# Pairs 4 and 5 in the form of the later pairs, in a kernel of chunked attention and a gated feed-forward layer

## The chip, the cores and the metric

One core of one Trainium2 chip. The metric is the device time in microseconds, the median of several executions. The engines are named as in the profile: PE multiplies matrices, PEld loads its weights, DVE, ACT and POOL work on vectors, and SP here only issues DMA transfers.

## The reference

The first part is a recurrence over a sequence (4 batches, 8 heads, 768 steps, head size 32, state size 16). The second part is a feed-forward layer on its output (256 in, 1536 inside, 256 out, 3072 tokens).

```python
for c in range(nc):                                   # chunks of the sequence
    cum = np.cumsum(la, axis=-1)                      # la = log(a) of the chunk
    L = np.exp(cum[..., :, None] - cum[..., None, :]) * causal
    M = np.einsum('bhin,bhjn->bhij', Cc, Bc) * L
    y_intra = np.einsum('bhij,bhjd->bhid', M, xc)
    y_inter = np.einsum('bhin,bhnd->bhid', Cc, state) * np.exp(cum)[..., None]
    y[:, :, sl] = y_intra + y_inter
    Bx = np.einsum('bhjn,bhjd->bhjnd', Bc, xc) * decay_from_j[..., None, None]
    state = decay_full[..., None, None] * state + np.sum(Bx, axis=2)
...
gate = np.maximum(x @ w_gate, 0.0)                    # x: y as (3072, 256)
return (gate * (x @ w_val)) @ w_out
```

## The kernel before

**Tiles.** The kernel cuts the sequence into chunks of 128 steps, six in a batch, and takes two chunks as a pair: 12 pairs of 256 tokens, three in a batch. A batch boundary lies ahead of pairs 3, 6 and 9. Two pairs are one block of 512 tokens for the feed-forward part, so there are six blocks. The decay of `a` is not put into the matrix: B is divided and C multiplied by the running product of `a` since the batch's middle (`fac`, and `wfac` for the first four pairs). What is carried over that point is multiplied by `over`.

**One pair.** B and C are loaded (`bcr`), x is loaded (`xr`) and cast (`xb`, `to_x`). Then come these steps:

- G: C times B for each head, into four PSUM banks; `gevac` masks it and writes it to SBUF (`gs`). For this B and C must lie with the state on the partitions, that is, turned.
- the states: B times x, summed over the chunks (`A_ps`, the PSUM bank with the tag `Aps`).
- `inter`: the carried term, C times the state, into y.
- `Dm`: `gs` times x, added into the same y. `yevac` writes y to `yT`, the input of the feed-forward part.

**Three forms.** Pairs 0 to 3 are wide (`NWIDE`): a load takes two neighbouring steps at once, B and C are scaled into `bs` (`scale_bc`), PE turns them (`turn`), ACT and DVE copy the result (`tevac`), and B is turned back (`back`). Pairs 4 and 5 are scaled into `bs` too and turned by PE, in the plain order of steps. Their states come from `states`, which adds up in PSUM, and `spread_one` on DVE multiplies out each chunk's carried term. Pairs 6 to 11 take a third form (`NDMA = 6`): POOL scales B and C into one of three zero-padded buffers (`scale_padded`: one product, two copies), and a DMA transpose that SP issues turns them into `TT`. `G_rows` and `inter_rows` read `TT` in strips of 32 rows. `states_two` makes the states of two pairs. `sums_two` adds them up chunk by chunk: a sum on DVE (`run`, L708 or L710), then a product on POOL (`Sn`, L717). At the fourth chunk of a batch (`c % NC == NC - 3`) POOL first multiplies the sum by `over` (L713), and the next sum on DVE adds that result:

```python
if c % NC == NC - 3:
    past = att.tile([128, 64], FP32, tag="run", name="run", bufs=4)
    nc.gpsimd.tensor_scalar_mul(past, total, over2[:, c // NC:c // NC + 1])
    total = past
running[:] = [total]
```

**Order.** Each engine, and SP's and POOL's DMA queues too, takes its instructions in the order in which the program writes them (`in_order`). The loop over blocks (L963) writes that order by hand. In block `b`, `P = 2b + 2` and `Q = 2b + 3` are the pairs of the next block, whose attention is worked on while block `b`'s feed-forward part runs. `gv` makes one of 12 slices of gate and value for 512 tokens (L738); ACT applies relu (L741) and DVE multiplies (L742). `gvh` does the same for 256 tokens (L753, L760, L763), so that a block can start while its second pair is not done: blocks 0, 1 and 2 do their first 4, 6 and 8 slices in halves. `fout` makes the output of 128 tokens from the 12 slices (L783), and `foevac` copies and stores it. With `apart` set, `fout` puts its first bank where `A_ps` lies (tag `Aps`, one buffer). From block 2 on the tail is the third form: `fout` 9 slices, `G_rows(P)`, `inter_rows`, and so on, down to `Dm_two` and `states_two` of the next two pairs. Blocks 0 and 1 have tails of their own.

**Loads.** SP issues nearly all of them, in program order: C, B and x of a pair by `load`. `held` and the memsets on `bcr` or `xr` make a load wait until DVE comes to them. `bcr` and `xr` have four buffers each, `TT` four, `xb` six.

Of the kernel before, what the change touches and what calls it, by code (L numbers as in the profile page):

```python
# [29 lines left out]
def kernel(  # L30
# [84 lines left out]
    even = const.tile([128, 24], FP32)  # L115
    even_att = att.tile([128, 32], FP32, bufs=1)
# [136 lines left out]
    over2 = const.tile([128, NB], FP32)  # L253
# [6 lines left out]
    def over_sum(de):  # L260
        own = smask.rearrange("p t (q d) -> p (t q) d", q=4)[:, :, 0]
        prod = const.tile([128, NB, 8], FP32)
        nc.vector.tensor_tensor(
            out=prod, in0=de.rearrange("p (b h) -> p b h", b=NB),
            in1=own.rearrange("p (o h) -> p o h", o=1).to_broadcast([128, NB, 8]),
            op=ALU.mult)
        nc.vector.tensor_reduce(out=over, in_=prod, op=ALU.add, axis=mybir.AxisListType.X)

    def over_sum2(de):
        own = smask.rearrange("p t (q d) -> p q t d", q=4)[:, :, :, 0]  # L270
        prod = const.tile([128, 2, 8], FP32)
        for n in range(2):
            nc.vector.tensor_tensor(
                out=prod[:, n].rearrange("p (q t) -> p q t", t=2),
                in0=de[:, (2 + n) * 8:(3 + n) * 8].rearrange("p (q t) -> p q t", t=2),
                in1=own, op=ALU.mult)
        nc.vector.tensor_reduce(out=over2[:, 2:4], in_=prod, op=ALU.add,
                                axis=mybir.AxisListType.X)
# [4 lines left out]
    NDMA = 6  # L283
# [24 lines left out]
    def new_bs(p):  # L308
        st[p]["bs"] = att.tile([128, 4, 128], BF16, tag="bs", name="bs", bufs=6)
        bs = st[p]["bs"]  # L310
        if p < NWIDE:
            st[p]["tin"] = [[bs[:, 2 * j + r] for r in range(2)] for j in range(2)]
        else:
            st[p]["tin"] = [[bs[:, 2 * i + j] for i in range(2)] for j in range(2)]
            st[p]["B"] = st[p]["tin"][0]
# [4 lines left out]
    def views(p, js):  # L320
        s = st[p]
        dst = s["bs"].rearrange("s k (q t n) -> s k t q n", q=4, t=2)
        if p < NWIDE:
            ks = slice(2 * js.start, 2 * js.stop)
            src = s["bcr"].rearrange("s (t q) j r n -> s (j r) t q n", t=2)
            return src[:, ks], dst[:, ks]
        return s["bcr"].rearrange("s i j (t q) n -> s (i j) t q n", t=2), dst

    def cast_bc(p, eng, js):
        src, dst = views(p, js)  # L330
        for t in range(2):
            copy(eng, dst[:, :, t], src[:, :, t])

    def scale_bc(p, eng, js=slice(0, 2), f=None, ts=(0, 1)):
        b, c0, _ = place(p)
        src, dst = views(p, js)
        if f is None:
            if p < NWIDE:
                f = wfac[:, p, js].rearrange("s j r h -> s (j r) h")
            else:  # L340
                f = fac[:, b, c0:c0 + 2].rearrange("s c j h -> s (c j) h")
        n = f.shape[1]
        for t in ts:
            eng.tensor_tensor(  # L344
                out=dst[:, :, t], in0=src[:, :, t],
                in1=f[:, :, 4 * t:4 * t + 4].to_broadcast([128, n, 4, N]), op=ALU.mult)

    def scale_one(p, eng, j):

        b, c0, _ = place(p)  # L350
        for i in range(2):
            f = fac[:, b, c0 + i, j].rearrange("s (t q) -> s t q", t=2)
            eng.tensor_tensor(
                out=st[p]["bs"][:, 2 * i + j].rearrange("s (q t n) -> s t q n", q=4, t=2),
                in0=st[p]["bcr"][:, i, j].rearrange("s (t q) n -> s t q n", t=2),
                in1=f.to_broadcast([128, 2, 4, N]), op=ALU.mult)

    def to_x(p, eng, f=None):
        xb = att.tile([128, 2 * NH * D], BF16, tag="xb", name="xb", bufs=6)
        xr = st[p]["xr"].rearrange("s i h d -> s (i h) d")  # L360
        out = xb.rearrange("s (k d) -> s k d", d=D)
        if f is None:
            copy(eng, out, xr)
        else:
            eng.tensor_tensor(out=out, in0=xr, in1=f.to_broadcast([128, 2 * NH, D]),
                              op=ALU.mult)
        st[p]["x"] = [xb[:, i * NH * D:(i + 1) * NH * D] for i in range(2)]

    def scale(p, eng):
        if p >= NDMA:  # L370
            scale_padded(p, eng)
        else:
            new_bs(p)
            scale_bc(p, eng)
        to_x(p, eng)
# [15 lines left out]
    def bevac(p, eng):  # L391
# [3 lines left out]
        if p < NWIDE:  # L395
            src = src.rearrange("s r m -> s m r")
            dst = dst.rearrange("s (m r) -> s m r", r=2)
        else:
            src = src.rearrange("s i m -> s (i m)")
        copy(eng, dst, src)  # L400
# [16 lines left out]
    def ct(p, i, rows=slice(0, 128), t=None):  # L417
        if p < NWIDE:
            c = st[p]["CT"][rows, :, :, 64 * i:64 * i + 64]
        else:  # L420
            c = st[p]["CT"][rows, :, i]
        return c if t is None else c[:, t]

    def split(p, ap):

        return ap.rearrange("s t (r m) -> s t r m", r=2) if p < NWIDE else ap
# [17 lines left out]
    def G(p):  # L444
# [4 lines left out]
        for i in range(2):  # L449
            for q in range(4):  # L450
                r = slice(32 * q, 32 * q + 32)
                nc.tensor.matmul(  # L452
                    out=split(p, g[q][:, i]), lhsT=s["BT"][r, i], rhs=ct(p, i, r),
# [100 lines left out]
    chunks = {}  # L554

    def states(p):
        c0 = 2 * (p % PPB)
        last = c0 + 2 == NC
        chunks[p] = (st[p]["B"], st[p]["x"])
        todo = [(0, p, 0)]  # L560
        if c0 and not last:
            todo.insert(0, (0, p - 1, 1))
        if not last:
            todo += [(1, p, 0), (1, p, 1)]
        for n, (k, e, i) in enumerate(todo):
            B_, x_ = chunks[e]
            xi = x_[i].rearrange("s (t q d) -> s q t d", t=2, q=4)
            for q in range(4):
                nc.tensor.matmul(
                    out=A_ps[0][32 * q:32 * q + 32, 0, 64 * k:64 * k + 64].rearrange(  # L570
                        "p (t d) -> p t d", t=2),
                    lhsT=B_[i][:, 32 * q:32 * q + 32], rhs=xi[:, q],
                    start=(n == 0 and (c0 == 0 or last)), stop=True,
                    tile_position=(0, 32 * q),
                    skip_group_check=True)

    def spread(p):
        for k in range(1 if 2 * (p % PPB) + 2 == NC else 2):
            S[2 * p + k + 1] = spread_one(2 * p + k + 1, k)

    def y_bank(s, apart=False):
        if "y" not in s:
# [4 lines left out]
            else:  # L587
                y = mm.tile([128, 2, 2, 128], FP32, tag="y", name="y")
                s["y"] = [y[:, 0], y[:, 1]]
                s["ya"] = y  # L590
# [8 lines left out]
    def inter(p, i):  # L599
# [5 lines left out]
        for t in range(2):  # L605
# [10 lines left out]
            out = s["y"][t][:, i]  # L616
            if p < NWIDE:
                out = out.rearrange("s (r m) -> s r m", r=2)
            nc.tensor.matmul(  # L619
                out=out, lhsT=Sm[:, t], rhs=ct(p, i, t=t),  # L620
# [16 lines left out]
    def yevac(p, *engs):  # L637
        s = st.pop(p)
        dst = yT[:, :, p * 256:(p + 1) * 256]
        if p >= NWIDE:  # L640
# [515 lines left out]
```

## Time and profile before

| | |
|---|---|
| time, median of 3 runs | 122.87 us (122.82 to 123.05) |
| the profiled execution: time, span | 123.24 us, 121.5 us |
| busy: PE, DVE, ACT, POOL | 117.3, 89.6, 73.8, 52.1 us |
| blocks on PE: 1, 2, 3 start at | 31.41, 49.64, 67.95 us |
| block 1's first `fout` starts at | 43.17 us |
| DMA transposes | 6, the first issued at 46.37 us |

The span is the profiled execution's time from its first to its last instruction; its own time is longer by what lies around the span. In a timeline a row is one or several instructions of a line of the kernel: start, busy time, engine, line, operation, tiles, and in brackets how long the engine idled just before and who ended that. The time of a DMA row is how long its issue held the queue. When its data have landed is a number of its own. Ends of matmuls are modelled, so the busy times of two neighbours overlap, and a step's cost is read from one start to the next.

### The profile page before, as it was taken

The page shows a single profiled execution, that of the slowest core. Times are in us where ns is not written, and L with a number is a line of the kernel's source. Part 1 is how long each engine was busy: PE and PEld are TensorE (multiplying, and loading weights), DVE is VectorE, ACT ScalarE, POOL GpSimd, SP SyncE. Part 2 cuts the span into 40 slices and gives each one's busy share as a digit, 9 for nine tenths or more (in the row PEclk, how much of TensorE's full clock was granted, in tenths as well). Part 3 has the DMA queues.
Part 4 walks back from the last instruction along what each step waited for, and adds up shares of the span by engine and source line. Part 5 has one row for each costly group of instructions (what it writes and reads, how often), then busy time and mean ns, then how long its engine had stood idle before and what let it go on. Part 6 is the DMA issues. An engine that isn't in the chain of part 4 may idle for free.

```text
span 121.5 us, 3331 instructions
## 1 busy us (share of the span) xinstructions
PE 117.3 (97%) x1238; PEld 75.3 (62%) x1238; DVE 89.6 (74%) x214; ACT 73.8 (61%) x160; POOL 52.1 (43%) x105
## 2 busy tenths in 40 slices
PE   7999999999999999999999999999999999999990
PEld 2446854676786477888477644578544677444790
DVE  5978878986999956899876588765778766578500
ACT  4177886840898734888744767625767445776340
POOL 6879999842615073768058252633400033000000
PEclk9999999999999999999999999999999999999999
DMA  3999999959997999799996799941300002200022
GB/s 59 212 195 172 191 197 206 187 86 126 165 105 157 98 125 154 91 131 218 117 148 139 73 127 113 291 94 58 115 0 5 0 0 92 86 0 0 0 86 86
DMA packets 80591, 13.69 MB, mean 113 GB/s; under 512 B 73424, under 2 KB 80576, under 8 KB 80576
## 3 DMA queue, kind: packets, MB, share of 16 engines
q1 hardware_dynamic: 73088, 10.54, 55.4%
q0 software_dynamic: 4080, 2.36, 13.8%
q10 hardware_dynamic: 3408, 0.59, 2.6%
q8 instruction: 9, 0.15, 0.6%
q14 instruction: 6, 0.05, 0.1%
HBM read 11.12 MB, written 3.15 MB: 117 GB/s over the span
## 4 chain that ended last, share of the span: by engine, by line
PE 93%; DVE 4%; issue 0%; DVEq 0%
PE o L783 25%; PE val L738 19%; PE gate L738 19%; PE gv L753 13%; PE w L200 4%; PE g L452 2%; PE g L491 2%; PE y L678 1%; PE y L630 1%; PE o L795 1%; PE tp L389 1%; DVE gs L475 1%; DVE CT L415 1%; DVE Sm L546 1%; PE y L619 1%; DVE bs L344 1%
## 5 line engine op out<-in xcount | busy, mean ns | idle before, releaser
L742 DVE TENSOR_TENSOR h<-r,val 128x512 bf16<-128x512 bf16 x54 | 36.9, 687 | 9.3 <-ACT r L741 6.4
L741 ACT ACTIVATE r<-gate 128x512 bf16<-128x512 f32 x54 | 32.3, 597 | 12.1 <-PE gate L738 11.3
L783 PE MATMUL o<-wo,h 128*128 128x256 bf16 x276 | 33.5, 273 | 0.0
L738 PE MATMUL val<-yT,wv 128*128 128x512 bf16 x108 | 32.6, 379 | 0.0
L738 PE MATMUL gate<-yT,wg 128*128 128x512 bf16 x108 | 32.6, 379 | 0.0
L783 PEld LDWEIGHTS <-h 128*128 128x128 bf16 x276 | 25.8, 98 | 5.4 <-issue 1.2
L171 POOL TENSOR_SCALAR_AFFINE_SELECT gs<-gs 128x512 bf16<-128x512 bf16 (+1 forms) x24 | 12.2, 533 | 22.1 <-ACT gs L464 22.1
L475 DVE TENSOR_TENSOR gs<-g,masks 128x512 bf16<-128x512 f32 x24 | 15.4, 685 | 6.0 <-PE g L491 2.8
L738 PEld LDWEIGHTS <-wv 128*128 128x128 bf16 x108 | 10.4, 98 | 12.8 <-DMA wv<-in_moe_w_val_dram 0.8
L738 PEld LDWEIGHTS <-wg 128*128 128x128 bf16 x108 | 10.4, 98 | 11.1
L464 ACT CAST gs<-g 128x512 bf16<-128x512 f32 x12 | 7.0, 587 | 15.7 <-PE g L452 7.3
L763 DVE TENSOR_TENSOR h<-r,gv 128x256 bf16<-128x256 bf16 x36 | 13.9, 417 | 0.9 <-ACT r L760 0.7
L760 ACT ACTIVATE r<-gv 128x256 bf16<-128x256 f32 x36 | 13.6, 388 | 1.2
L753 PE MATMUL gv<-yT,wg 128*128 128x256 bf16 x72 | 13.9, 273 | 0.0
L753 PE MATMUL gv<-yT,wv 128*128 128x256 bf16 x72 | 13.8, 273 | 0.0
L297 POOL TENSOR_TENSOR bz<-bcr,fac 128x512 bf16<-128x512 f32 x6 | 6.4, 1060 | 11.7 <-DMA bcr<-in_B_dram 9.4
L811 ACT COPY ob<-o 128x512 f32<-128x512 f32 x11 | 6.5, 592 | 4.1 <-PE o L783 4.0
L318 ACT CAST yT<-y 128x512 bf16<-128x512 f32 (+1 forms) x9 | 4.6, 528 | 5.4 <-PE y L678 3.4
L318 POOL CAST xb<-xr 128x512 bf16<-128x512 f32 (+1 forms) x10 | 6.0, 597 | 4.2 <-DMA xr<-in_x_dram 3.1
L753 PEld LDWEIGHTS <-wv 128*128 128x128 bf16 x72 | 7.0, 98 | 0.8
L753 PEld LDWEIGHTS <-wg 128*128 128x128 bf16 x72 | 6.7, 98 | 1.1 <-issue 0.2
L200 PE MATMUL w<-const-bfloat16-1.0 128*128 128x512 bf16 (+3 forms) x16 | 6.2, 511 | 0.8 <-PEq L1140 0.8
(119 smaller groups left out, 110.5 us busy)
## 6 DMA issues: line engine op xcount, KB each, us to landing
xr<-in_x_dram SPq DMA_DIRECT2D x23, 128.0 KB, 3.3
out_dram<-ob SPq DMA_DIRECT2D x9, 256.0 KB, 2.7
bcr<-in_B_dram SPq DMA_DIRECT2D x16, 64.0 KB, 3.0
bcr<-in_C_dram SPq DMA_DIRECT2D x16, 64.0 KB, 3.0
wg<-in_moe_w_gate_dram POOLq DMA_DIRECT2D x6, 128.0 KB, 5.5
wv<-in_moe_w_val_dram POOLq DMA_DIRECT2D x6, 128.0 KB, 5.4
wo<-in_moe_w_out_dram POOLq DMA_DIRECT2D x3, 256.0 KB, 6.9
out_dram<-ob SPq DMA_DIRECT2D x4, 128.0 KB, 2.2
```

The source lines that it names most:

```text
L171: nc.gpsimd.affine_select(out=dst, in_=dst, pattern=pattern, compare_op=ALU.is_ge, fill=0.0, base=0, channel_multiplier=-1)
L200: nc.tensor.matmul(out=w[:, 0:cols], lhsT=nc.const_aps.tensor(1.0, [128, 128], BF16), rhs=nc.const_aps.tensor(1.0, [128, cols], BF16), sta ...
L318: (eng.copy if eng is nc.scalar else eng.tensor_copy)(out=out, in_=in_)
L464: nc.scalar.copy(out=d[:, 0], in_=g[0])
L475: nc.vector.tensor_tensor(out=d[:, q], in0=g[q], in1=m, op=ALU.mult)
L738: nc.tensor.matmul(out=o, lhsT=w_tile(ws, f, k), rhs=yT[:, k, tk], start=(k == 0), stop=(k == 1), skip_group_check=True)
L741: nc.scalar.activation(r, g, AF.Relu)
L742: nc.vector.tensor_tensor(out=fst[b][:, f], in0=r, in1=v, op=ALU.mult)
L753: nc.tensor.matmul(out=gv_[:, j], lhsT=w_tile((wgs, wvs)[j], f, k), rhs=yT[:, k, tk], start=(k == 0 and not (early and j)), stop=(k == 1), ...
L760: nc.scalar.activation(r[:, 0:256], fst[b, f, u][:, 0], AF.Relu)
L763: nc.vector.tensor_tensor(out=fst[b][:, f, u * 256:(u + 1) * 256], in0=fst.pop((b, f, u, "r"))[:, 0:256], in1=fst.pop((b, f, u))[:, 1], op ...
L783: nc.tensor.matmul(out=o[:, ts % 2], lhsT=fst[b][:, f, ts * 128:(ts + 1) * 128], rhs=wo[:, f], start=(f == 0 and new), stop=(f == NF - 1), ...
```

## The change

Pairs 4 and 5 take the third form too: scaled by POOL into the padded buffers, turned by DMA transposes, with `G_rows`, `inter_rows`, `Dm_two`, `states_two` and `sums_two`. The code that only they used goes out (`states`, `spread`, `scale_one`, `over_sum2`, `over2`). Pair 3 stays wide, but its heads take their natural order, so that its states (`states_two((3,))`) and its carried term (`inter_wide`) are in the order of the later pairs, and the chain of sums starts with it. `over_sum` makes `over` for all batches in two orders of heads. Block 1 now ends with the tail of the later blocks. Its states and sums come after slices 8, 9 and 10 (`g` 0, 1 and 2), with `scale(6)` and the load of pair 8 after the first of them. In block 2 all slices are whole; the states of pairs 6 and 7 come after slice 4, their sums after slices 4 to 7. Pair 4's load goes out in the order C, B, x; pair 5's is no longer held by a memset; the cast of pair 3's x goes from POOL to ACT; the stores of blocks 2 and 3 are in one piece.

The core of the diff:

```diff
-    NDMA = 6
+    NATURAL = 3
...
     def scale(p, eng):
-        if p >= NDMA:
-            scale_padded(p, eng)
-        else:
-            new_bs(p)
-            scale_bc(p, eng)
+        scale_padded(p, eng)
         to_x(p, eng)
...
+    def inter_wide(p, i, opened):
+
+        Sm = S.pop(2 * p + i)
+        for t in range(2):
+            for q in range(4):
+                r, o = slice(32 * q, 32 * q + 32), 64 * (q % 2)
+                nc.tensor.matmul(
+                    out=Y[q // 2][o:o + 64, p % 2, i].rearrange("s (r m) -> s r m", r=2),
+                    lhsT=Sm[r], rhs=ct(p, i, r, t=t), start=q not in opened, stop=True,
+                    tile_position=(32 * q, o), skip_group_check=True)
+                opened.add(q)
...
-    def sums_two(ps):
+    def sums_two(ps, ns=range(4)):
 
         A = A_ps[0].rearrange("p a d -> p (a d)")
         for n, (p, i) in enumerate(todo(ps)):
+            if n not in ns:
+                continue
...
-                nc.gpsimd.tensor_scalar_mul(past, total, over2[:, c // NC:c // NC + 1])
+                nc.gpsimd.tensor_scalar_mul(past, total, over[:, c // NC:c // NC + 1])
...
         if b == 1:
-            load(P + 2, nc.sync)
+            new_bc(P + 2)
+            load_bc(P + 2, 1, nc.sync)
+            load_bc(P + 2, 0, nc.sync)
+            scale(Q, nc.gpsimd)
+            new_x(P + 2)
+            for i in range(2):
+                load_x(P + 2, i, nc.sync)
             load(P + 3, nc.sync)
...
-        nh = (4, 6, 8, 0)[min(b, 3)]
+        nh = (4, 6, 0)[min(b, 2)]
...
+            if f == 3:
+                opened = y_banks()
+                inter_wide(W, 1, opened)
+                Dm_two((W,))
+                yevac_wide(W, nc.scalar)
...
-            elif b == 1:
-                if f == nh:
-                    turn(P)
-                    tevac(P, nc.scalar, nc.vector)
-                    scale(Q, nc.gpsimd)
-                if f == 8:
-                    turn(Q)
-                    tevac(Q, nc.scalar, nc.vector)
-                    scale(Q + 1, nc.gpsimd)
-                    load(Q + 3, nc.sync)
-            elif b == 2:
-                if f == 9:
+            elif b < 3:
+                g = f - (8 if b == 1 else 4)
+                if g == 0:
+                    states_two((P, Q))
+                    sums_two((P, Q), (0,))
+                    scale(P + 2, nc.gpsimd)
+                    if b == 1:
+                        load(Q + 3, nc.sync)
+                elif g > 0:
+                    sums_two((P, Q), (g,))
+                if b == 2 and f == 9:
...
-            held(Q + 2)
+            load(Q + 2, nc.sync)
...
+            Dm(P)
+            states_two((Q,))
+            yevac(P, nc.vector)
+            G(Q)
+            gevac(Q, after={3: lambda: sums_two((Q,))})
+            scale(Q + 1, nc.gpsimd)
+            fout(b, 3, range(6, NF))
+            foevac(b, 3)
         elif more:
-            ahead = (P + 2, Q + 2) if Q + 2 < NPAIR else ()
+            ahead = (P + 2, Q + 2) if 1 < b and Q + 2 < NPAIR else ()
```

The old tail of block 1 (`fout(b, 0)`, `G(P)`, ..., `Dm(P)`, `states(Q)`, `yevac`, `G(Q)`, `spread(Q)`) goes out, and block 1 takes the `elif more` branch. In block 0 the order of the tail stays but for the lines shown.

More of the change, by code (lines that the diff above doesn't have):

```diff
@@ L345, in scale_bc, with to_x @@
                 out=dst[:, :, t], in0=src[:, :, t],
[L346 to L358, printed above, removed]
-        xb = att.tile([128, 2 * NH * D], BF16, tag="xb", name="xb", bufs=6)
[L360 to L366, printed above, removed]
+                in1=f[:, :, t].to_broadcast([128, n, 4, N]), op=ALU.mult)
+    def to_x(p, eng):
+        xb = att.tile([128, 2 * NH * D], BF16, tag="xb", name="xb", bufs=6)
+        copy(eng, xb.rearrange("s (k d) -> s k d", d=D),
+             st[p]["xr"].rearrange("s i h d -> s (i h) d"))
         st[p]["x"] = [xb[:, i * NH * D:(i + 1) * NH * D] for i in range(2)]
     def scale(p, eng):
-        if p >= NDMA:
-            scale_padded(p, eng)
-        else:
-            new_bs(p)
-            scale_bc(p, eng)
+        scale_padded(p, eng)
         to_x(p, eng)
@@ L550, in spread_one @@
         return n
[L554 to L579, printed above, removed]
     def y_bank(s, apart=False):
@@ L811, in foevac @@
         nc.scalar.copy(out=ob, in_=o or fst["o"])
-        rows = out[r0 - 128:r0 + 128, :].rearrange("(i p) m -> p i m", p=128)
-        for part in ((slice(0, 1), slice(1, 2)) if b in (2, 3) and ts == 3 else (slice(0, 2),)):
-            nc.sync.dma_start(out=rows[:, part], in_=ob[:, part])
+        nc.sync.dma_start(
+            out=out[r0 - 128:r0 + 128, :].rearrange("(i p) m -> p i m", p=128), in_=ob)
     B_, C_ = slice(0, 1), slice(1, 2)
@@ L952 @@
         gvh_mul(0, f, 0)
-    nc.scalar.copy(out=de, in_=de_ps)
     for w in range(W3):
@@ L1045 @@
                     nc.vector.memset(st[Q + 1]["bcr"][0:1, 0, 0, 0, 0:1], 0.0)
[L1046 to L1050 removed]
+                    load(Q + 1, nc.sync)
                     for n in range(1, NB):
@@ L1059 @@
             foevac(b, 1)
+            to_x(Q, nc.scalar)
             fout(b, 2)
```

148 lines of the change are left out of this document (29 added, 119 removed).

## The prediction

> **What bounds the kernel now.** I read the page's busy table and its chain that ended last first, then the timeline of PE from 26 to 90 us, then the timelines of SP, POOL and DVE over block 1 (31 to 50 us), and the landing times of single loads.
>
> ```profile
> PE 117.3 (97%) x1238; PEld 75.3 (62%) x1238; DVE 89.6 (74%) x214; ACT 73.8 (61%) x160; POOL 52.1 (43%) x105
> PE 93%; DVE 4%; issue 0%; DVEq 0%
> ```
>
> PE is the chain. From 30 to 110 us it never idles, so every PE step removed shortens the span and every wait that is put on PE lengthens it by its whole length. The other engines matter only if PE comes to wait for them. The steps of pairs 4 and 5 and of the later form, on PE (start, busy; I cost a step from its start to the next start):
>
> ```profile
> 38.18 0.39 PE L389 MATMUL tp<-ident,bs 128*128 128x128 bf16 x4
> 40.13 0.39 PE L389 MATMUL tp<-ident,bs 128*128 128x128 bf16 x4
> 42.94 0.39 PE L619 MATMUL y<-CT,Sm 128*128 128x128 bf16 x4
> 44.57 0.40 PE L452 MATMUL g<-CT,BT 32*128 32x256 bf16 x8
> ...
> 61.94 0.42 PE L491 MATMUL g<-TT 32*64 32x256 bf16 x16
> 62.19 0.35 PE L665 MATMUL y<-TT,Sn 32*64 32x128 bf16 x12
> ```
>
> SP's queue, which issues nearly all loads, is the second thing to read. It is full from 24 to 61 us: one transfer after the other, with no gap over 0.2 us between 26 and 53 us.
>
> ```profile
> 37.67 1.19 SPq L92 DMA_DIRECT2D bcr<-in_C_dram  x2
> 38.91 1.51 SPq L92 DMA_DIRECT2D bcr<-in_B_dram  x2
> 40.51 1.36 SPq L100 DMA_DIRECT2D xr<-in_x_dram  x2
> ...
> 46.37 2.41 SPq L306 DMA_TRANSPOSE TT<-bz  x1
> 48.83 1.20 SPq L92 DMA_DIRECT2D bcr<-in_C_dram  x2
> ```
>
> The three load rows are pair 6. Its second x half was issued at 41.09 and landed 3.1 us later, at 44.19. POOL had long been waiting:
>
> ```profile
> 42.87 1.06 POOL L297 TENSOR_TENSOR bz<-bcr,fac 128x512 bf16<-128x512 f32 x1 [3.19 <-DMA bcr<-in_B_dram]
> 43.99 0.53 POOL L303 COPY bz<-bz 128x128 bf16<-128x128 bf16 x2
> 44.46 0.62 POOL L318 CAST xb<-xr 128x512 bf16<-128x512 f32 x1
> ```
>
> That is `scale(6)`. Today no PE step waits for that, since block 1's carried term is made by DVE alone. So the 3.19 us cost nothing.
>
> **What PE gains.** Removed before block 1's `fout` (which now starts at 43.17): 4 of the 12 matmuls of pair 3's states (0.06), states of pair 4 (0.22), two `turn`s (0.44), `inter` of pair 4 (0.23). Added: `states_two((4, 5))`, 12 matmuls, 0.19 as at 84.75. `inter_wide(3, 1)`, 8 small matmuls for 2 large, comes to 0.2 either way (12 of such a shape took 0.28 at 62.19). PE would reach `fout(1, 0)` at 43.17 - 0.95 + 0.19 = 42.41. From there to the block's end it took 6.47; out go G of both pairs (0.66), Dm of pair 4 (0.23), states of pair 5 (0.13); in come `G_rows` twice (0.25 + 0.35), 16 matmuls of `inter_rows` (0.33), `Dm_two` (0.46): 6.84. Block 2 took 18.31; `inter` and Dm of pair 5 go (0.32 + 0.23), and eight half tiles become whole (0.873 against 0.865 each, 0.07): 17.69. The rest, from 67.95 to the end, is 53.55. If nothing waits, the span is 42.41 + 6.84 + 17.69 + 53.55 = 120.5, or 1.0 less than now.
>
> **Where PE will wait.** In block 1 the new order after `gv` 8 is: `states_two((4, 5))`; the sum of chunk 8 on DVE; `scale(6)` on POOL; after `gv` 9 the sum of chunk 9, with its multiplication by `over` on POOL; after `gv` 10 the sum of chunk 10 on DVE, which adds that POOL result. POOL takes its queue in order. So the multiplication stands behind `scale(6)`, whose last step casts pair 6's x. DVE's sum of chunk 10 waits for it, with the multiplication of `gv` 11 queued behind. And it is the last reader of the `Aps` bank, which `fout(1, 0)` now takes. PE stops there. The link is in the trace already, in block 3, where the same multiplication holds DVE (two views, POOL and DVE):
>
> ```profile
> 86.23 0.44 POOL L713 TENSOR_SCALAR run<-run,over 128x64 f32<-128x64 f32 x1
> 86.70 0.23 DVE L708 TENSOR_TENSOR run<-A_ps,run 128x64 f32<-128x64 f32 x1 [0.58 <-POOL run L713]
> ```
>
> From landing of x to PE: 0.14 to the cast's start, 0.62 cast, 0.04, 0.45 multiplication, 0.03, 0.23 sum, about 0.13 to PE: 1.64 us. With pair 6's x at 44.19 as today, PE resumes at 45.83, 3.4 us late.
>
> But x lands later. The change puts pair 4's transpose on SP ahead of pair 6's B and C, and pair 5's between those and x. SP has no slack there. A transpose holds SP for 1.23 to 2.41 us (six rows). What follows it is late by more: the row at 46.37 delays the next load 2.46; that at 54.24 took 1.30, but the C load behind it took 1.66 instead of some 0.4. I take 2.4 each, the nearest rows, since all of them stand between loads; the ends are 1.3 and 2.6. Both source buffers are ready earlier (POOL finishes pair 4 near 35, pair 5 at 37.63 + 1.06 + 0.53 = 39.2; SP comes by at 37 and 42.8). So x(6) lands at 44.19 + 4.8 = 49.0 and PE resumes at 50.63.
>
> The Trainium skill (Advanced Engine Details and Errata, X-Bar Transpose) says a transposing DMA on trn2 is as fast as an ordinary one. By that each would cost about the 0.91 us of SP that the 256 KB store at 30.63 took, and the time would come out near 129; the rows above disagree with it, and it stands beside the second rival.
>
> **Restart.** PE then sits idle 8 us. After the first 10 us no row of PE shows an idle of over 0.4 us. But the start shows what PE does when it comes from rest:
>
> ```profile
> 0.83 3.04 PE L200 MATMUL w<-const-bfloat16-1.0 128*128 128x512 bf16 x7 [0.83 <-PEq L1140]
> ...
> 67.95 0.38 PE L738 MATMUL gate<-yT,wg 128*128 128x512 bf16 x1
> 68.17 0.38 PE L738 MATMUL val<-yT,wv 128*128 128x512 bf16 x1
> ```
>
> There 512 columns take 434 ns, later 216 (starts 67.95 and 68.17); at 10.22 it is at full speed, and the rows before it change over near 7.2. The page's granted clock says full in both. So a restart costs between 0 and half of 6.4, 3.2 us; I take the middle, 1.6. The Trainium skill (TensorE: Matmul & The Clock Gate, part 1) has PE at half rate after about 3.4 us idle, for about 3.4 us, so an estimate of 1.7 in place of 1.6; no run here shows it in mid-kernel.
>
> **Edits at nothing.** `to_x(3)` on ACT: ACT idles 3.18 us before its G copy at 30.77. `over_sum` over all batches: one more 0.12 us DVE step in block 0, one ACT copy less. Pair 3's sums: two POOL products of 0.29 that end near 32.9, PE comes at 33.1; if the cover is gone, some tenths. Pair 5's cast ends at 39.9 and PE wants it at 39.6: 0.3. Both tenths fall ahead of the large wait and vanish in it. Block 2's states and sums move to whole tiles: the POOL multiplication is last there and no DVE step reads it before the block's end. `scale(8)` comes earlier in the block, with loads that will have had 8 us more to land. Stores in one piece instead of two: SP only.
>
> **Sum.** 50.63 + 6.84 + 17.69 + 53.55 + 1.6 = 130.3 of span against 121.5: +8.8. The profiled execution took 123.24 for its span of 121.5, 0.37 above the median of 122.87; the outside does not change, so 122.87 + 8.8 = 131.7.
>
> **Rivals.**
> - *Cheap transposes.* Same wait, but each transpose delays what follows only by its own median issue, 1.31. PE resumes at 48.45, span 126.5 to 128.1 with the restart: 127.9 to 129.5. For it: at 63.80 a transpose took 1.23. Against: two rows where the followers were late. If they cost nothing at all: 45.83, +2.4, 125.3.
> - *Faster: POOL is through in time.* If x of pair 6 lands early enough that the multiplication is done when DVE gets to chunk 10, only the saving stays: 121.9. It decides at a landing of about 41, for PE to go on at 42.41. Against it: today's 44.19 with fewer transfers ahead in the same full queue. It would need SP to run 3 us ahead of today.
> - *Longer.* x behind pair 5's transpose lands as slowly as x(3) and the loads of pair 5 did (4.3 and 4.4 instead of 3.1), and the restart costs the full 3.2: PE at 52.0, 134.7.
> - *The change does not do what it says:* if the sum of chunk 10 did not hold `Aps`, DVE would still stand, and `gv` 11's product with it, until the same moment; PE could go only 9 `fout` and some `G_rows` further, about 1.3 us less wait.
>
> **How the numbers follow.** Forecast 0.55; cheap or free transposes 0.26; longer 0.12; faster 0.06, the last 0.01 at no change. About 0.2% is what a measurement of this kernel can tell from no change. The range takes the forecast, the cheap case and most of what lies between the forecast and the longer case: 126.5 to 134.5. Slower 0.93, faster 0.06, same 0.01.
>
> **What would show it.** PE idle of 6 to 9 us ending near 50 us, just ahead of block 1's first `fout`, put down to DVE's `run` step; that step waiting for POOL's multiplication by `over`, which follows the cast of pair 6's x, which waits for a load; two transposes on SP before that load; matmuls at double spacing for some us after. PE steps outside it shorter by about 1.0 in all. If PE shows no idle there, or the cast of x(6) ends before 42, the forecast is wrong; if the transposes' followers on SP start under 1.5 us later, the cheap case holds.

## The result, and the profile after

The changed kernel takes 130.34 us, the median of six executions (129.74 to 132.7), against 122.86 us before: a ratio of 1.0602, 95% interval 1.0554 to 1.065. The forecast was 131.7 us in a range of 126.5 to 134.5: the time lies inside the range, 1.4 us below the forecast. The profiled execution took 129.74 us with a span of 128.0. (Ratios leave out single disturbed executions, medians and lowest-to-highest do not, so a ratio can differ a little from the quotient of two medians.)

The page: the busy line, the engines' shares of the chain that ended last, and PE's busy time and granted clock in 40 slices.

```profile
PE 117.2 (92%) x1208; PEld 71.6 (56%) x1216; DVE 86.6 (68%) x198; ACT 71.7 (56%) x148; POOL 54.3 (42%) x111
PE 76%; SPq 9%; DMA 4%; DVE 4%; issue 2%; POOL 1%; ACT 1%; POOLq 0%; DVEq 0%
PE   7889999999997409999999999999999999999991
PEclk9999999999999995999999999999999999999999
```

PE is busy as long as before (117.2 us for 117.3), but its share of the span has fallen from 97% to 92%. The chain, which was 93% PE, now runs through SP's queue and the DMAs. There is one hole, in slices 14 and 15 (of 3.2 us each), and the slice behind it runs at half the clock. PE's timeline at that place:

```profile
40.22 0.21 PE L621 MATMUL A_ps<-xb,bz 128*32 128x64 bf16 x4 [0.66 <-POOL xb L305]
42.53 0.59 PE L668 MATMUL val<-yT,wv 128*128 128x512 bf16 x2
48.07 2.10 PE L713 MATMUL o<-wo,h 128*128 128x256 bf16 x9 [4.95 <-DVE run L638]
50.10 0.65 PE L434 MATMUL g<-TT 32*64 32x256 bf16 x16
```

PE finishes block 1's last slice at about 43.1 and waits 4.95 us for a DVE sum before its first `fout`. POOL, then DVE, then SP show why:

```profile
43.78 1.06 POOL L289 TENSOR_TENSOR bz<-bcr,fac 128x512 bf16<-128x512 f32 x1 [2.71 <-DMA bcr<-in_B_dram]
46.71 0.62 POOL L305 CAST xb<-xr 128x512 bf16<-128x512 f32 x1 [1.28 <-DMA xr<-in_x_dram]
47.31 0.45 POOL L643 TENSOR_SCALAR run<-run,over 128x64 f32<-128x64 f32 x1
```
```profile
47.79 0.22 DVE L638 TENSOR_TENSOR run<-A_ps,run 128x64 f32<-128x64 f32 x1 [4.60 <-POOL run L643]
```
```profile
36.61 1.33 SPq L298 DMA_TRANSPOSE TT<-bz  x1
38.05 0.52 SPq L742 DMA_DIRECT2D out_dram<-ob  x1
...
41.60 1.25 SPq L298 DMA_TRANSPOSE TT<-bz  x1
42.90 1.20 SPq L100 DMA_DIRECT2D xr<-in_x_dram  x2
```

Read from the end: PE at 48.07 behind the sum of chunk 10; the sum behind the multiplication by `over` on POOL; that behind `scale(6)`, whose cast waits for pair 6's x; and x in SP's queue behind both new transposes. Its second half was issued at 43.52 (41.09 before) and landed 3.1 us later, at about 46.62, against 44.19 before.

The span grew by 6.5 us: block 1 starts 0.70 earlier (30.71 for 31.41), it is 7.79 longer (26.02 for 18.23), block 2 is 0.53 shorter (17.78 for 18.31), the rest 0.06 shorter.

### The profile page after: what moved, and what is told of

Same layout as the page of the kernel before. It is cut to its first block, busy times and chain, and to the rows that moved or that the text cites. A ratio compares the mean times of both kernels' runs of the same rounds, so it can differ in the third digit from the quotient of the medians.

```text
span 128.0 us, 3255 instructions
## 1 busy us (share of the span) xinstructions
PE 117.2 (92%) x1208; PEld 71.6 (56%) x1216; DVE 86.6 (68%) x198; ACT 71.7 (56%) x148; POOL 54.3 (42%) x111
## 3 DMA queue, kind: packets, MB, share of 16 engines
HBM read 11.12 MB, written 3.15 MB: 111 GB/s over the span
## 4 chain that ended last, share of the span: by engine, by line
PE 76%; SPq 9%; DMA 4%; DVE 4%; issue 2%; POOL 1%; ACT 1%; POOLq 0%; DVEq 0%
PE o L713 25%; PE gate L668 19%; PE val L668 18%; SPq L92 4%; PE gv L683 3%; DMA xr<-in_x_dram 2%; PE g L434 2%; SPq L100 2%; DMA a_sb<-in_a_dram 2%; SPq L298 2%; PE y L606 2%; PE g L395 1%; PE o L725 1%; DVE bs L318 1%; DVE gs L418 1%
## 5 line engine op out<-in xcount | busy, mean ns | idle before, releaser
L672 DVE TENSOR_TENSOR h<-r,val 128x512 bf16<-128x512 bf16 x62 | 42.1, 687 | 12.2 <-ACT r L671 8.1
L671 ACT ACTIVATE r<-gate 128x512 bf16<-128x512 f32 x62 | 37.0, 597 | 15.8 <-PE gate L668 14.5
L668 PE MATMUL gate<-yT,wg 128*128 128x512 bf16 x121 | 36.9, 379 | 0.2
L668 PEld LDWEIGHTS <-wv 128*128 128x128 bf16 x124 | 12.1, 98 | 14.4
L668 PEld LDWEIGHTS <-wg 128*128 128x128 bf16 x124 | 11.9, 98 | 13.2
L693 DVE TENSOR_TENSOR h<-r,gv 128x256 bf16<-128x256 bf16 x20 | 7.8, 416 | 0.9 <-ACT r L690 0.7
L690 ACT ACTIVATE r<-gv 128x256 bf16<-128x256 f32 x20 | 7.6, 388 | 0.6
L305 DVE CAST yT<-y 128x256 bf16<-128x256 f32 (+1 forms) x8 | 4.4, 567 | 5.1 <-PE y L606 3.1
L683 PE MATMUL gv<-yT,wg 128*128 128x256 bf16 x40 | 7.8, 273 | 0.0
L683 PE MATMUL gv<-yT,wv 128*128 128x256 bf16 x40 | 7.7, 272 | 0.0
## 6 DMA issues: line engine op xcount, KB each, us to landing
xr<-in_x_dram SPq DMA_DIRECT2D x23, 128.0 KB, 3.2
wg<-in_moe_w_gate_dram POOLq DMA_DIRECT2D x6, 128.0 KB, 4.7
wv<-in_moe_w_val_dram POOLq DMA_DIRECT2D x6, 128.0 KB, 4.9
bcr<-in_C_dram SPq DMA_DIRECT2D x3, 128.0 KB, 3.5
```

The costliest lines, as they stand in the source:

```text
L305: (eng.copy if eng is nc.scalar else eng.tensor_copy)(out=out, in_=in_)
L668: nc.tensor.matmul(out=o, lhsT=w_tile(ws, f, k), rhs=yT[:, k, tk], start=(k == 0), stop=(k == 1), skip_group_check=True)
L671: nc.scalar.activation(r, g, AF.Relu)
L672: nc.vector.tensor_tensor(out=fst[b][:, f], in0=r, in1=v, op=ALU.mult)
L683: nc.tensor.matmul(out=gv_[:, j], lhsT=w_tile((wgs, wvs)[j], f, k), rhs=yT[:, k, tk], start=(k == 0 and not (early and j)), stop=(k == 1), ...
L690: nc.scalar.activation(r[:, 0:256], fst[b, f, u][:, 0], AF.Relu)
```

## The experiments

The theory was that PE's wait is all there is: POOL's multiplication standing behind `scale(6)`, with the transposes setting how long. The rivals were that the wait goes elsewhere once its link is cut, and that the two transposes cost time by themselves. Twelve kernels were run. Each diff is against the changed kernel unless it says otherwise; code lines are shortened.

### 1. `scale(6)` and the load of pair 8 behind the sums

```diff
                 if g == 0:
...
-                    scale(P + 2, nc.gpsimd)
-                    if b == 1:
-                        load(Q + 3, nc.sync)
+                    if b == 2:
+                        scale(P + 2, nc.gpsimd)
                 elif g > 0:
                     sums_two((P, Q), (g,))
+                    if b == 1 and g == 2:
+                        scale(P + 2, nc.gpsimd)
+                        load(Q + 3, nc.sync)
```

> The changed kernel, but in block 1 scale(6) and pair 8's load stand behind the sums of chunks 9 and 10 (after slice 10) instead of ahead of them (after slice 8). Theory: PE's wait of 5.0 us ahead of block 1's first fout comes from POOL's queue alone, because the multiplication by over stands behind scale(6). Then DVE's sum of chunk 10 runs right after slice 10, the wait and the 1.7 us of half rate go, and the time falls from about 130 to 122.3 to 123.4; POOL's two masks of pairs 4 and 5 now stand behind scale(6) and may hold Dm_two by up to 0.8, and the 0.7 us wait for pair 5's cast stays. Rival: pair 6's late x is wanted by something else too (a bank, a buffer, SP), and a wait of over 2 us turns up elsewhere: 125 or more.

Measured: 125.79 us, ratio 1.0214 (1.0152 to 1.0276). The wait at block 1's first `fout` fell from 4.95 to 0.25 and the clock stayed full: the link is shown. But the run did not come down to the time before; its time is the rival's. Of the missing part, 0.86 us is PE's wait for the cast of pair 5's x in block 1, which run 5 takes up. Most of the rest lies in block 2 (POOL, then PE):

```profile
65.75 1.06 POOL L289 TENSOR_TENSOR bz<-bcr,fac 128x512 bf16<-128x512 f32 x1 [5.35 <-DMA bcr<-in_B_dram]
...
67.91 1.97 POOL L171 TENSOR_SCALAR_AFFINE_SELECT gs<-gs 128x512 bf16<-128x512 bf16 x4
```
```profile
68.61 0.60 PE L606 MATMUL y<-gs,xb 128*32 128x128 bf16 x8 [0.58 <-POOL gs L171]
69.57 0.82 PE L606 MATMUL y<-gs,xb 128*32 128x128 bf16 x24 [0.36 <-POOL gs L171]
```

The first row is `scale(9)`. Pair 9's load was issued at 58.29, before the change at 55.59: 2.7 later, by the two transposes ahead in the queue. `scale(9)` stands ahead of the four masks of block 2's `gs`, and `Dm_two` needs those. Before the change (POOL, then PE):

```profile
64.67 1.97 POOL L171 TENSOR_SCALAR_AFFINE_SELECT gs<-gs 128x512 bf16<-128x512 bf16 x4
```
```profile
66.85 0.63 PE L678 MATMUL y<-gs,xb 128*32 128x128 bf16 x32
```

There the masks ended at 66.64 and `Dm_two` came 0.2 us later, so nothing was seen of it. Here they end at 69.9. Without a wait `Dm_two` would come as far behind the start of the `fout` ahead of it as before (2.18 us), at 67.96; the `fout` behind it starts at 70.41, so this part takes 2.45 us instead of 0.65, some 1.8 more. In the changed kernel, PE's 4.95 us in block 1 had given the load queue time to catch up: there the masks end at 73.05 and `Dm_two` comes at 73.41. The two waits hide one another.

### 2. The multiplication by `over` on DVE

```diff
-                nc.gpsimd.tensor_scalar_mul(past, total, over[...])
+                (nc.vector if c == 9 else nc.gpsimd).tensor_scalar_mul(past, total, over[...])
```

> The changed kernel with one edit: at chunk 9 the multiplication by over is done by DVE instead of POOL. scale(6) stays where it is. Theory: all that POOL has queued behind scale(6) is late until its cast ends near 47.3, so the wait only moves: fout(1, 0) starts near 43.2, PE stops at inter_rows(5), which wants the products Sn of chunks 9 and 10 from POOL, and goes on near 48.0 with 1.3 us of work already done. Time 127.0 to 128.7. Rival: only the link from POOL's multiplication to DVE's sum and the Aps bank holds PE; with it gone the whole wait and the restart go: about 123.

The four times reach from 125.33 to 128.31 (median 127.83, inside the theory's range) and give no ratio; the profiled execution was the fastest. Its first `fout` starts at 43.15, behind 0.48 us. The wait moves one step on, to `inter_rows(5)`, which reads a product (`Sn`) that POOL makes behind the same cast:

```profile
46.40 0.50 PE L574 MATMUL y<-TT,Sn 32*64 32x128 bf16 x8 [1.63 <-POOL Sn L647]
```

PE goes on at 46.40 and not near 48.0, as pair 6's cast began at 45.48 here (46.71 in the changed kernel). So it is not one instruction: everything that POOL does for pairs 4 and 5 after slice 8 stands behind pair 6's load.

### 3. Both new transposes behind pair 6's x on SP

```diff
+        if p > 5:
             nc.sync.dma_start_transpose(out=tt, in_=...)
...                                    # block 1, behind load_x(6)
+            for p in (P, Q):
+                nc.sync.dma_start_transpose(out=st[p]["TT"], in_=turned[p % 3]...)
```

> The changed kernel, but SP issues both new transposes (pairs 4 and 5) behind pair 6's x instead of ahead of its B and C and of its x. Nothing else moves. Theory: each transpose holds up what follows by its own issue, 1.3 us, so pair 6's B and C land 1.3 and its x 2.6 us earlier; POOL's cast then follows its own copies without a wait, and PE goes on near 45.5 instead of 48.07. With a wait of only 2.5 us the half rate may stay away: time 125.6 to 127.5. The prediction's price of 2.4 each would give 4.8 us earlier at x, which POOL's own work would cut to about the same 45.5 or a little less. Rival: the queue is paced by the loads themselves and the transposes ran in time that was free: PE goes on at 47.5 to 48, time 129.5 to 130.

Measured: 127.62 us, ratio 1.0376 (1.0327 to 1.0425).

```profile
45.64 1.16 PE L714 MATMUL o<-wo,h 128*128 128x256 bf16 x9 [3.15 <-DVE run L639]
```

PE goes on at 45.64, which is 2.43 earlier than with the transposes in front, just what the change had put x(6) off by; at 36.5 SP stood at the same point in both (36.49 here, 36.61 there). So the two transposes together put off PE's return by 2.4 us. The wait itself is only 1.80 shorter, as PE also got there 0.64 earlier. The rest of it is there because pair 6's x lands about 44 even without them, and the cast, at 44.28, follows POOL's own copies. The hope that the half rate would stay away failed (last section), and the time is 0.1 above the theory's range.

### 4. PE kept busy during the wait

Added work: 22 matmuls of 512 columns whose result nobody reads, ahead of block 1's `fout`.

```diff
+            if b == 1:
+                warm = mm.tile([128, 512], FP32, tag="y", name="warm")
+                for _ in range(22):
+                    nc.tensor.matmul(out=warm, lhsT=ones, rhs=ones, start=True, stop=True)
```

> The changed kernel with 22 matmuls of 512 columns on constants ahead of block 1's first fout; they write a free bank that nothing reads, and fill 4.75 of the 5.0 us in which PE waits. Theory: the wait itself stays (PE goes on with fout near 48.1), but PE does not come from rest, so the first fout and G run at full rate: 1.7 us less than the changed kernel, near 128.2. Rival: the slow rows after the wait are not a matter of rest but of what runs there (weights, banks, other engines catching up): no gain, 129.7 to 130.

Measured: 127.52 us, ratio 1.0397 (1.0358 to 1.0436).

```profile
47.13 1.14 PE L713 MATMUL o<-wo,h 128*128 128x256 bf16 x9
48.20 0.42 PE L434 MATMUL g<-TT 32*64 32x256 bf16 x16
```

The clock is 1.00 throughout. The first nine `fout` matmuls take 1.07 us from their start to the next step; in the changed kernel 2.03. From the first `fout` to block 2 it is 7.13 us here and 8.66 there. So the restart costs about 1.5 us. The rest of the gain in time does not come from the added matmuls by any row: SP was 0.82 us ahead already at the C load of pair 5 (30.45 for 31.27), where nothing differs yet, and pair 6's cast started at 45.59 here and at 46.71 there. Why is not shown.

### 5. The states of pair 5 later too

Run 1, and `states_two` of block 1 in two parts, pair 5's after slice 9, as `to_x(5)` ends late:

```diff
-                    states_two((P, Q))
+                    states_two((P, Q), range(2) if b == 1 else range(4))
...
+                    if b == 1 and g == 1:
+                        states_two((P, Q), (2,))
```

> The changed kernel with scale(6) and pair 8's load behind the sums (as in the first experiment) and pair 5's states one slice later: states_two of pair 4 after slice 8, of pair 5 after slice 9. Theory: the 0.7 to 0.9 us in which PE waited for the cast of pair 5's x go, and nothing takes their place in block 1; the 2.1 us at block 2's Dm_two stay, since they come from SP's queue: 124.2 to 125.0, against 124.5 to 126.1 for the first experiment. Rival: the queue sets the pace of all, so what is won in block 1 is lost again in block 2: no gain, 125 to 126.

Measured: 125.06 us, ratio 1.0158 (1.0108 to 1.0209). The wait for pair 5's cast (0.86 in run 1) is gone. What stays is 0.25 at the first `fout`, and block 2's `Dm_two` at 67.17, which takes 1.18 us up to the next `fout` instead of 0.65 (66.85 to 67.50 before the change). The median lies on the border between the ranges of theory and rival, and its interval overlaps run 1's, so the gain over run 1 is seen in the rows only.

### 6. The two transposes alone, in the kernel before

Against the kernel before; the two transposes are added work, from a buffer that lies ready into one that nobody reads.

```diff
+            nc.sync.dma_start_transpose(out=spare, in_=turned[2]...)   # block 0's tail
...
+            nc.sync.dma_start_transpose(out=spare, in_=turned[2]...)   # between pair 6's B and x
```

> The kernel before with one addition: two DMA transposes of a zero buffer into a spare tile that nothing reads, at the two places on SP where the change puts its own (behind pair 5's load, and between pair 6's C and x). No other engine has more or less to do. Theory: each delays SP by 1.3 to 1.45, so pair 9's load is 2.7 later and POOL's masks of block 2, which stand behind scale(9) and ended 0.2 ahead of need, hold Dm_two by 2.0 to 2.6: 124.8 to 125.4. Rival: the kernel before has room on its queue and nothing waits: 122.8 to 123.2.

Measured: 124.63 us, ratio 1.0133 (1.0088 to 1.0178), about 1.6 us. They held SP for 1.32 and 1.30 us, and pair 9's load went out at 57.92 (55.59 before). POOL and PE:

```profile
46.53 0.64 POOL L318 CAST xb<-xr 128x512 bf16<-128x512 f32 x1 [1.10 <-DMA xr<-in_x_dram]
47.13 1.00 POOL L171 TENSOR_SCALAR_AFFINE_SELECT gs<-gs 128x512 bf16<-128x512 bf16 x2
```
```profile
47.82 0.71 PE L630 MATMUL y<-gs,xb 128*32 128x128 bf16 x16 [0.35 <-POOL gs L171]
```

Pair 6's cast comes at 46.53, much as in the changed kernel (46.71), where it began at 44.46 before. Here only the masks of pair 4 stand behind it, so 2.07 us of lateness cost PE 0.35 of wait at that place, and the product there takes 0.49 up to the next step instead of 0.23. At block 2's `Dm_two`, where the theory had 2.0 to 2.6, it is 0.2. Other starts move by tenths; in the profiled execution all of it comes to 1.1 us of span. So the two transposes do cost time by themselves, but not where they were expected to.

### 7 and 8. x of pairs 5 and 6 on ACT's DMA queue

Run 1 (and, in 8, run 5) with four loads of x off SP's queue:

```diff
-            for i in range(2):
-                load_x(P + 2, i, nc.sync)
...
+                if b == 1 and f in (6, 7):
+                    load_x(P + 2, f - 6, nc.scalar)
...                                    # block 0's tail, for pair 5
+            for i in range(2):
+                load_x(Q + 2, i, nc.scalar)
```

> The first experiment's kernel (scale(6) behind the sums), with the x of pairs 5 and 6 issued from ACT's DMA queue, pair 5's in block 0's tail ahead of the cast of pair 3, pair 6's one half each after slices 6 and 7 of block 1. SP is so relieved of four issues, about what the two new transposes take from it. Theory: SP's issue sets the pace, 1.3 to 1.45 us for a transpose and 0.6 to 0.7 for half a load; then load 9 is back at its old time, block 2's Dm_two no longer waits, and the time falls by some 2 to 3 us to 122 to 123.3. Rival: the 16 DMA engines are full (busy share about 1.0) and a second queue only shares them: no gain, 124.5 to 126, and the loads on SP take longer each.

> All three moves together: scale(6) behind the sums, pair 5's states one slice later, x of pairs 5 and 6 on ACT's queue. Theory: no wait is left of those that the change brought, and its saving on PE of about 1.0 stays: 121.6 to 122.3, below the kernel before. Rival: the DMA engines are the limit: 124 to 125.

Measured: 127.16 us, ratio 1.0336 (1.0281 to 1.039), and 129.51, ratio 1.0531 (1.0485 to 1.0577). Both are worse, and neither decides the question, as ACT's own queue stopped (run 7):

```profile
41.90 0.39 ACTq L100 DMA_DIRECT2D xr<-in_x_dram  x1
42.39 0.60 ACT L671 ACTIVATE r<-gate 128x512 bf16<-128x512 f32 x1 [4.30 <-DMA bcr<-in_B_dram]
```

By the profile, ACT's first issue started when a B load of SP's queue had come in, and its second, at 43.55, when pair 5's transpose had (issued at 40.49, landed 3.03 later). The relu stood behind the issue, and PE waited 2.3 us for the relu; in run 8 it waited 2.6 and 1.9 us. Why ACT waits for SP's transfers is not shown. What can be read is SP's side, run 7 against run 1: 2.71 us of issue (x of pair 5) was taken off it, and the transpose behind it went out 0.98 sooner (35.83 for 36.81), as the B load of pair 5 took 2.72 instead of 1.53 and x of pair 4 took 2.16 instead of 1.44.

### 9, 10 and 11. The sums a slice earlier, with the queue in three versions

The states of pair 4 and the sum of chunk 8 after slice 7, the others after 8 and 9, `scale(6)` behind them; in run 9 and 10 pair 7's transpose behind pair 9's load, in run 10 and 11 x of pair 5 alone on ACT.

```diff
+                if b == 1:
+                    if f == 7:
+                        states_two((P, Q), range(2))
+                    if f == 9:
+                        states_two((P, Q), (2,))
+                    if f in (7, 8, 9):
+                        sums_two((P, Q), (f - 7,))
+                    if f == 9:
+                        scale(P + 2, nc.gpsimd)
...
```

> The fifth kernel, moved further: in block 1 pair 4's states stand after slice 7, pair 5's after slice 9, the sums of chunks 8 to 10 after slices 7 to 9, scale(6) and pair 8's load behind them; in block 2 SP issues pair 7's transpose behind pair 9's load instead of ahead of it. Theory: the 0.45 us at block 1's first fout go, and pair 9's load comes 1.3 earlier, so that block 2's masks no longer hold Dm_two: 122.0 to 123.2, at or just below the kernel before (122.9). Rival: the queue of loads is simply too full, and x of pair 5 or 6 or the masks of block 1 hold PE instead, by 1 us or more: 124 to 125.

> The same kernel with pair 5's x issued from ACT's queue in block 0's tail (where ACT is idle) instead of from SP. Theory A, SP's issue sets the pace: all loads after it are 2.3 us earlier, and no wait for a load is left: 121.5 to 122.3. Theory B, the DMA engines set the pace: the loads around it take longer, later ones gain under 1 us, and the time is that of the kernel without this move within 0.5 us.

> The run of before with pair 5's x on ACT's queue, with one thing put back: pair 7's transpose stands ahead of pair 9's load again, as in the changed kernel. In the run before it, issued behind that load at 60.36, it cost 1.59 us of PE's wait in the combining of pair 7's rows, which read its result first. Theory (the load queue is the rest of the cost): SP's issues of block 2 come 1.3 to 2.2 us sooner than with every load on SP, so the masks of block 2 are in time again, PE waits less than 0.4 us in blocks 1 and 2 together, and the run takes 121.5 to 122.6 us, the time before or a little under it. Rival (pair 9's load is the cost, wherever the queue stands): GpSimd's scaling of pair 9 again holds the masks of block 2, PE waits 0.8 to 2 us at the first diagonal product there, and the run takes 123.5 to 124.5 us.

Measured: 128.8 us, ratio 1.0403 (1.0363 to 1.0442); 125.21, ratio 1.0194 (1.0159 to 1.0229); 127.49, ratio 1.0233 (1.0159 to 1.0306). Block 1 is free of the large wait in all three (first `fout` at 42.90 and 42.82 in the first two). In 9 and 10 the transpose was put too far back: `inter_rows(7)` reads it before `G_rows(7)` does, and PE waited 3.31 us for it in run 9, with half rate behind that (granted 0.50 over 65 to 69 us), and, in run 10,

```profile
63.80 0.30 PE L575 MATMUL y<-TT,Sn 32*64 32x128 bf16 x8 [1.59 <-DMA TT<-bz]
```

Put back in run 11, that wait is gone, and the masks hold `Dm_two` again (0.62 and 0.36 us), with pair 9's load at 60.17. Its profiled execution had half rate from about 7.5 to 14.3 us and reached block 1's `fout` only at 45.45, so its total says little; its waits say that the rival named there was right. One x load on the second queue let SP's later issues go 1.3 to 2.2 us sooner (run 10 against 9: pair 6's C at 37.41 for 38.84), out of 2.67 us of issue taken off, which lies between run 10's two theories (2.3, and under 1).

### 12. The masks of pair 6 ahead of `scale(9)`

The order of run 11 in block 1, every load on SP, pair 7's transpose as in the changed kernel, and:

```diff
-                if b == 2 and f == 9:
-                    scale(Q + 2, nc.gpsimd)
-                    load(Q + 3, nc.sync)
-                    load(Q + 4, nc.sync)
...
             gevac(P)
+            if b == 2:
+                scale(Q + 2, nc.gpsimd)
+                load(Q + 3, nc.sync)
+                load(Q + 4, nc.sync)
             fout(b, 0, range(9, NF))
```

> The changed kernel with three of its orders mended and every load on SP's queue: the pair states of block 1 a slice earlier with those of pair 5 after slice 9, pair 6's scaling and pair 8's load behind the last sum, and (new here) pair 9's scaling, with the two loads behind it, after pair 6's masks instead of ahead of them. Theory (what is left of the loss is that the masks of block 2 stand behind pair 9's scaling, whose load comes late): pair 6's masks run from about 63.4, the scaling behind them, pair 7's masks end at about 67.6 where 67.83 was seen before, but only the second half of the diagonal products needs those; PE waits less than 0.3 us in block 1's and in block 2's output phases, and the run takes 122.5 to 123.6 us, that is no more than 0.6 per cent from the kernel before: the change's own gain of a microsecond is then still missing. Rival (the load queue itself costs it, in whatever order GpSimd works): another product of block 2 or 3 waits in its place and the run takes 124 to 125.5 us.

Measured: 123.97 us (123.3 to 126.83), ratio 1.0095 (1.0057 to 1.0132). The profiled execution, the fastest, took 123.30 with a span of 121.6. PE, then POOL:

```profile
42.70 1.15 PE L716 MATMUL o<-wo,h 128*128 128x256 bf16 x9
...
66.64 0.93 PE L606 MATMUL y<-gs,xb 128*32 128x128 bf16 x32
```
```profile
62.91 1.01 POOL L171 TENSOR_SCALAR_AFFINE_SELECT gs<-gs 128x512 bf16<-128x512 bf16 x2 [3.58 <-ACT gs L407]
63.89 1.07 POOL L289 TENSOR_TENSOR bz<-bcr,fac 128x512 bf16<-128x512 f32 x1
...
66.06 1.00 POOL L171 TENSOR_SCALAR_AFFINE_SELECT gs<-gs 128x512 bf16<-128x512 bf16 x2
```

Now the first masks no longer wait for pair 9, `Dm_two` takes 0.95 up to the next `fout` (0.65 before the change, 1.18 in run 5), and the largest wait on PE that the profile lists behind the first 25 us is 0.34. The profiled execution is where the theory had it. The median is 0.4 above the theory's range and a little below the rival's, so what the other executions lose stays open: only one of them has a profile. Of all versions this is the nearest to the time before, and none beats it.

## Why the prediction was right, and where it was not

**The mechanism: right.** The wait was forecast ahead of block 1's first `fout`, put down to DVE's `run` step, behind POOL's multiplication, behind the cast of pair 6's x, behind a load, behind two transposes on SP. The rows above show each link. Run 1 cuts it at POOL and run 3 shortens it at SP. Two of the signs that the prediction named came out smaller: the wait is 4.95 us and ends at 48.07 (6 to 9 us near 50 were forecast), and PE's steps outside it are shorter by 0.5 to 0.7 us, not 1.0. From the landing of x to PE the prediction added up 1.64 us; it was about 1.45 (46.62 to 48.07).

**The mis-sized term: the transposes.** The prediction took 2.4 us each, the value of the row at 46.37, and 4.8 together. Measured: 1.44 and 1.30 from their start to the next issue, nothing behind them late by more, and x(6) later by 2.43 altogether. By the prediction's own sign, followers late by less than 1.5 us, this is the case that stood as a rival, "cheap transposes": 48.45 for PE's return; 48.07 was measured, and 50.63 forecast. The forecast span of 130.3 is 2.3 above the 128.0 measured: 2.56 too much at PE's return, less some 0.25 that the later blocks took above their terms; x's landing (46.62, not 49.0) is 2.38 of the 2.56. That the median came nearer to the forecast (130.34 for 131.7) than the span is luck: the profiled execution was the fastest of the six. The cause is in how the row was read. It is the transpose of pair 6, and the same instruction took 1.24 in run 7, 1.41 in run 12, 1.90 in run 11 and 2.35 in run 2. That speaks for a queue that was full at that moment and not for the price of a transpose; what the long issue waited for, no row shows. The Trainium skill (Advanced Engine Details and Errata, X-Bar Transpose) has a transposing DMA on trn2 as fast as an ordinary one. The 1.3 us here, beside the 0.91 of the store, is nearer to the page than my 2.4.

**The restart: right, by luck of the middle.** 1.6 was taken between 0 and 3.2. Run 4 gives 1.5 by difference, and against run 12, where the same stretch takes 7.26, the changed kernel's 8.66 gives 1.4. The middle itself had no row behind it. The prediction held that the page's granted clock says nothing of a restart; here it does. PE by windows of 1 us (length, PE busy, granted clock, DMA share, GB/s):

```profile
48.00:49.00 1.00, 0.93 (x5) 0.51 1.00 97
...
51.00:52.00 1.00, 1.00 (x15) 0.79 0.83 172
```

Half rate from 48 to about 51.4, 3.4 us. The Trainium skill (TensorE: Matmul & The Clock Gate, part 1) gives that length, from which the prediction had its estimate of 1.7 us lost. The trace agrees on the length. The work in it lost a little less, since it did not quite slow down twofold: nine `fout` matmuls took 2.03 us for run 4's 1.07, and the small matmuls of `G_rows` and `inter_rows` behind them 1.02 for 0.58.

**What PE gains: nearly twice too high.** Run 12 shows the steps almost without waits. Its first `fout`, less 0.34 of wait, would start at 42.36 (42.41 forecast). The tail of block 1 is 7.26 (7.13 in run 4), not 6.84: the 48 `fout` matmuls in four groups cost 5.64 where they had cost 5.45, and the rows of G, carried and diagonal products 1.62 where I had 1.39. Block 2, less its 0.3 of wait, is 17.78 (17.69 forecast), the rest 53.56 (53.55). Together 120.96: a gain of 0.5 us, or 0.7 with run 4's tail, not 1.0.

**A price that was not in the sum.** The rival "faster" priced the change at 121.9 if POOL were through in time. Runs 1, 5 and 12 brought that about and took 125.79, 125.06 and 123.97. The transposes delay every later load, and the next step with little slack, the masks behind `scale(9)`, had 0.2 us; it cost PE 1.8, 0.5 and 0.3 us in these runs. The prediction gave block 2 a saving and "8 us more to land", which held only while PE stood still in block 1. The transposes alone cost 1.6 us in the kernel before (run 6), more than the whole gain.

## What to carry to other kernels

When a step joins an engine that takes its work in order, look at what stands ahead of it in that queue and what that waits for: here a load for the pair after next held up sums that were ready. In a load queue with no gaps each new transfer costs every later load its length, and the price shows at the first consumer with no slack, so list the slacks of all of them (here 0.2 us at `Dm_two`) and not only the first wait. And take the price of a transfer from its shortest rows: here a transpose cost its followers 1.3 to 1.4 us, though single rows in a full queue showed up to 2.4.

## What the runs showed of the hardware that I had not expected

- PE fell to half rate after a wait of 3.15 us too (run 3). The clock was full on return at 45.64 and fell about 1.2 us later: granted 0.72 over 46 to 48 us and 0.50 over 48 to 50. The stretch to block 2 took 8.76 us, as long as after 4.95 us of waiting (8.66). A wait of 2.3 us ended so too (run 7: back at 43.04, granted 0.50 over 45 to 48 us); one of 1.63 us did not (run 2: 1.00 throughout). In run 9 the clock fell at about 64.6, ahead of PE's return at 65.98, so the fall is not tied to the return.
- In runs 7 and 8 a DMA issue on ACT held ACT, by the profile until a load from another queue had come in (idle times of 4.30 and 4.17 us).
- Taking transfers off a full queue gives back less than their issue time: 0.98 of 2.71 us (run 7), 1.3 to 2.2 of 2.67 (run 10). The Trainium skill (DMA: Bandwidth & Descriptors, Issuing engines are not separate DMA queues) says that all engines' DMAs run on the same 16 DMA engines. The B load that took 2.72 us instead of 1.53 in run 7 is in line with that; no run here takes the engines and the queue apart.
- With the same order on SP up to that point, pair 6's cast began at 46.71, 45.48, 45.59 and 47.10 in the changed kernel and runs 2, 4 and 1. Where PE waits for a load, such a spread goes into the time.
